# Moving a column minimum and the 1/l and h of two batches from VectorE to GpSimd in a fused attention and gated feed-forward kernel

## The chip, the cores and the metric

The kernel runs on one core of a Trainium2 chip. The metric is the device time of one execution in microseconds (us). A core has five engines that work side by side and wait for each other through semaphores: TensorE (PE in the profile, with its weight loads as PEld), VectorE (DVE), ScalarE (ACT), GpSimd (POOL) and SyncE (SP, which here only issues transfers). Each engine works through its own queue in the order in which the program wrote it.

## The reference

Two functions follow each other. The first is an attention through 32 inducing points, over 4 batches of 12416 tokens with 128 channels:

```python
def mab(q, kv):
    s = scale * (q @ kv.transpose(0, 2, 1))
    s = s - s.max(-1, keepdims=True)
    a = np.exp(s)
    a /= a.sum(-1, keepdims=True) + 1e-09
    return a @ kv
h = mab(I, x)          # stage 1: 32 points look at all tokens of a batch
return mab(x, h)       # stage 2: every token looks at the 32 points
```

The second is a gated feed-forward layer over all 49664 tokens, with 1536 hidden columns:

```python
gate = 1.0 / (1.0 + np.exp(-(x @ w_gate)))
val = x @ w_val
return (gate * val @ w_out).astype(np.float32)
```

## The kernel before, in words

Three things are interleaved. **The feed-forward steps** carry the program. The tokens go through in blocks of 512 (four chunks of 128). For each block 12 column groups of hidden values are made, in 8 steps that hold two groups (128x1024) and one group (128x512) in turn. For a step TensorE fills a gate tile and a value tile in PSUM (`hidden_mm`, L955), ScalarE takes the tanh of the gate tile (`gate`, L974), VectorE forms (t + 1) times the value tile (`product`, L987, written as `u`), and TensorE projects `u` with the output weights (`project`, L1018). The value and gate tiles have one PSUM buffer for the wide step and one for the narrow step. The weights of the gate and the values are folded with h beforehand: `hw_fill` (L426) multiplies h of a batch into both weight matrices, so that a block needs only the stage-2 probabilities of its tokens as the other operand.

**Stage 1 and stage 2 of later batches** run beside these steps, by a plan written out by hand. Two steps make a slot. `at(slot, f)` puts a piece of work behind the first step of a slot, and `at(slot, f, late=True)` behind the second. `beside` writes out what a slot has. A batch has 96 slots; in the code `b` counts from 0, and `o` is the first slot of the period in which the blocks of batch `b` go through. In that period the h of batch `b + 1` is made. The text calls the periods by their batches, 1 to 4.

- `plan_stage2` handles a group of 16 chunks: score by TensorE (`s2_score`, L533, which reads h as its moving operand), copy to SBUF by ScalarE (`s2_take`, L567), maximum and subtraction by a tree on GpSimd (`s2_lower_pool`, L577 to L584), exponential by ScalarE (`s2_exp_low`, L593), sum, inverse and product on GpSimd (`s2_sum_pool` L601, `s2_inverse_pool` L625 to L640, `s2_spread` L647), and a transposing transfer issued by SyncE (`s2_turn_dma`, L658). The inverse on GpSimd is a power with exponent -1 and one Newton step.
- `plan_combine` makes h of the next batch. Stage 1 leaves, for each row of 128, several columns of negated maxima (7 for batch 2, 5 for batches 3 and 4) and as many partial sums. `least` takes the minimum over the columns on VectorE (L469), and `join_min` joins the four row groups on GpSimd (L443 to L458). `weigh` makes the weights on ScalarE (L474), `join` adds the weighted sums on GpSimd (L485 to L493), `total` lets TensorE sum over the row groups into a PSUM tile `lh` (L505, L506) and takes the reciprocal of its l half on VectorE (L415), and the next slot multiplies the h half with it on VectorE (L420, `h_take`). The fills of `hw` follow 18 slots behind `join`.
- For batches 3 and 4 `least` stands at o + 44, `weigh` at o + 49, `join` at o + 54, `total` at o + 61, `h_take` at o + 62; for batch 2 at o + 52, 55, 56, 63 and 64.
- The first group of batch `b + 1` is scored in slots o + 67 and o + 68 (its `s2_score` is the first reader of the new h), copied at o + 70 and exponentiated at o + 78; the last group of batch `b` is copied at o + 58 and exponentiated at o + 66.
- `x_load` (L82) issues the input loads of batch `b + 2` from GpSimd's queue, in slots given at the end of the plan.

[...]

Of the kernel before, what the change touches and what calls it, by code (L numbers as in the profile page):

```python
# [9 lines left out]
F32 = mybir.dt.float32  # L10
# [3 lines left out]
ALU = mybir.AluOpType  # L14
AX = mybir.AxisListType

AFTER = mybir.DependencyInfo(mybir.DependencyClass.Sync, mybir.DependencyReason.DATA)
P = 128
GC = 16
# [7 lines left out]
def kernel(  # L27
# [9 lines left out]
    nc = tc.nc  # L37
    B, N, C = x.shape
    m = inducing.shape[0]
# [5 lines left out]
    NLO = NCH - NG * GC  # L45
# [10 lines left out]
    bp = ctx.enter_context(tc.tile_pool(name="bp", bufs=2))  # L56
    s1p = ctx.enter_context(tc.tile_pool(name="s1p", bufs=4))
    s2p = ctx.enter_context(tc.tile_pool(name="s2p", bufs=2))
    up = ctx.enter_context(tc.tile_pool(name="up", bufs=6))
    tp = ctx.enter_context(tc.tile_pool(name="tp", bufs=4))  # L60
    op = ctx.enter_context(tc.tile_pool(name="op", bufs=4))
# [12 lines left out]
    def x_load(b, s, first=0):  # L74
        c0, n = groups[s]
        if s == 0:
            c0, n = 0, n + NLO
        if b not in xn:
            xn[b] = xnp.tile([P, NCH, C], F16, tag="xn", name=f"xn_{b}")
        cuts = [c0, c0 + first, c0 + n] if first else [c0, c0 + n]  # L80
        for c, e in zip(cuts, cuts[1:]):
            nc.gpsimd.dma_start(xn[b][:, c:e, :], xv[b, :, c:e, :])  # L82
# [18 lines left out]
    def keep_on(n, tag):  # L101
# [14 lines left out]
        out=identf[:],  # L116
        in_=identf[:],
# [39 lines left out]
    minus1 = const.tile([P, GC + NLO], F32, tag="minus1")  # L157
# [36 lines left out]
    def at(slot, make, late=False):  # L194
        plan.setdefault((slot, late), []).append(make)
# [207 lines left out]
    hT16 = {}  # L403
# [9 lines left out]
    def l_inverse(l_ps):  # L413
        li = bp.tile([P, m], F32, tag="li")
        nc.vector.reciprocal(out=li[:], in_=l_ps)  # L415
        return li

    def h_take(b, h_ps, li):
        hT16[b] = bp.tile([P, m], F16, tag="hT", name="hT")
        nc.vector.tensor_tensor(out=hT16[b][:], in0=h_ps, in1=li[:], op=ALU.mult)  # L420

    def hw_fill(b, hf, tag):
        hw_ps = ps.tile([P, F // 4], F32, tag=tag, name="hw_ps")
# [37 lines left out]
    def plan_combine(b, lead, weights, joined, fill):  # L461
        q = b % 2
        nm1, hst = nm1s[q], hsts[q]
        st = {}
        ns = NS if b < 2 else NSH

        def least():
            ml = bp.tile([P, 1], F32, tag="ml")
            nc.vector.tensor_reduce(out=ml[:], in_=nm1[:, 0:ns], axis=AX.X, op=ALU.min)  # L469
            st["col"] = join_min(bp, ml)  # L470

        def weigh():
            st["w"] = bp.tile([P, NS], F32, tag="w1", name="w1")
            nc.scalar.activation(  # L474
                out=st["w"][:, 0:ns],
                in_=nm1[:, 0:ns],
                func=AF.Exp,
                bias=st["col"][:],
                scale=-1.0,
            )  # L480

        def join():
            assert summed[b] == ns
            hx = bp.tile([P, NS, C + 1], F32, tag="hx", bufs=1)
            nc.gpsimd.tensor_tensor(  # L485
                out=hx[:, 0:ns, :],
                in0=hst[:, 0:ns, :],
                in1=st["w"][:, 0:ns].unsqueeze(2).to_broadcast((P, ns, C + 1)),
                op=ALU.mult,
            )  # L490
            add_tree(hx, ns)
            e32l = bp.tile([P, m], F32, tag="e32l")
            nc.gpsimd.tensor_scalar(  # L493
                out=e32l[:],
                in0=e32[:],
                scalar1=hx[:, 0, C : C + 1],
                scalar2=TINY,
                op0=ALU.mult,
                op1=ALU.add,
            )  # L500
            st["hx"], st["e32l"] = hx, e32l

        def total():
            lh = ps.tile([P, 2, m], F32, tag="m", name="lh_ps")
            nc.tensor.matmul(lh[:, 0, :], ones[:], st["e32l"][:], start=True, stop=True)  # L505
            nc.tensor.matmul(lh[:, 1, :], st["hx"][:, 0, 0:C], e32[:], start=True, stop=True)  # L506
            st["lh"], st["li"] = lh, l_inverse(lh[:, 0, :])

        def part(hf):
            st["hw_ps"] = hw_fill(b, hf, "m")  # L510

        def keep(hf):
            if hf == 0:
                st["hwt"] = bp.tile([P, NI, P], F16, tag="hw", bufs=B, name="hwt")
            hw_take(st["hwt"], hf, st["hw_ps"])
            if hf == 1:
                hw[b] = st["hwt"]

        at(lead, least)
        at(weights, weigh)  # L520
        at(joined, join)
        at(joined + 7, total)
        at(joined + 8, lambda: h_take(b, st["lh"][:, 1, :], st["li"]))
        for hf, (first, second) in enumerate(fill):
            at(first, lambda hf=hf: part(hf))
            at(second, lambda hf=hf: keep(hf), late=True)
# [95 lines left out]
    def s2_inverse_pool(n, sme):  # L622
        rs = s2p.tile([P, GC + NLO], F32, tag="rs")
        near = s2p.tile([P, GC + NLO], F32, tag="near")
        nc.gpsimd.tensor_tensor(  # L625
            out=near[:, 0:n], in0=sme[:, 0:n], in1=minus1[:, 0:n], op=ALU.pow
        )
        off = s2p.tile([P, GC + NLO], F32, tag="off")
        nc.gpsimd.tensor_tensor(
            out=off[:, 0:n], in0=sme[:, 0:n], in1=near[:, 0:n], op=ALU.mult  # L630
        )
        nc.gpsimd.tensor_scalar(
            out=off[:, 0:n],
            in0=off[:, 0:n],
            scalar1=-1.0,
            scalar2=2.0,
            op0=ALU.mult,
            op1=ALU.add,
        )
        nc.gpsimd.tensor_tensor(  # L640
            out=rs[:, 0:n], in0=near[:, 0:n], in1=off[:, 0:n], op=ALU.mult
        )
        return rs[:, 0:n]

    def s2_spread(n, e, rs, eng):
# [94 lines left out]
    nm1, l1, hst = nm1s[0], l1s, hsts[0]  # L740
    for p in range(-2, NS - 3):
# [13 lines left out]
        if p == EARLY - 2:  # L755
            we = const.tile([P, EARLY], F32, tag="we")
            nc.vector.tensor_reduce(
                out=nml[:, 0:1], in_=nm1[:, 0:EARLY], axis=AX.X, op=ALU.min
            )
            nc.scalar.activation(  # L760
                out=we[:], in_=nm1[:, 0:EARLY], func=AF.Exp, bias=nml[:, 0:1], scale=-1.0
# [20 lines left out]
    c0, n = groups[sc]  # L782
# [3 lines left out]
    for j0, tag, copy in ((GC // 2, "v2", nc.scalar.copy), (GC - BC, "g1", nc.vector.tensor_copy)):  # L786
# [15 lines left out]
    ml = const.tile([P, 1], F32, tag="ml")  # L802
# [10 lines left out]
        out=top[:],  # L813
        in_=mlT_ps.rearrange("o (g r) -> o r g", g=4),
        axis=AX.X,
        op=ALU.min,
# [5 lines left out]
    for g in range(4):  # L822
# [19 lines left out]
        out=e32l[:], in0=e32[:], scalar1=lsum[:], scalar2=TINY, op0=ALU.mult, op1=ALU.add  # L842
# [5 lines left out]
        out=hw_parts[3],  # L848
# [195 lines left out]
    for b in range(B):  # L1044
        o = base[b]
        more = b + 1 < B

        if b == 0:
            plan_stage2(0, groups[1][0], o, None, o + 3, soon=True)
            plan_stage2(0, groups[2][0], o + 5, o + 7, o + 18)  # L1050
        for s in range(3 if b == 0 else 2, NG - 1):
            k = o + 16 * s - 28
            lag = k + 4 if b and more and s == 3 else None
            plan_stage2(b, groups[s][0], k, k + 2, k + (14 if more else 10), lag=lag)
        late = 2 if more and b else 0
        plan_stage2(b, groups[NG - 1][0], o + 56, o + 58, o + 66, far=o + 52 + late)
        if not more:
            continue
        single = (32, (47, 47, 47) if b else (43, 43, 43))
        if b == 0:  # L1060
            early = [(9, (16, 17, 17)), (13, (24, 24, 24))]
            later = [(25, (31, 31, 31)), (28, (35, 35, 35)), (40, (47, 48, 49)), (44, (50, 51, 51))]
            parts = dict(enumerate(early + later + [single]))
            turns = (5, 7, 17, 19, 22, 25, 20)
        else:
            parts = {2: (7, (16, 17, 17)), 3: (11, (18, 19, 19)), NG: single}
            turns = (-14, -5, -3, 2, 0, 8, 20)
            plan_shared(
                b + 1,
                o,  # L1070
                (-6, 2, 10, 14),
                (7, 11, 15),
                23,
                (26, 30, 42, 46),
                (40, 42, 49, 51),
                (45, 53),
            )
        for s, (score, total) in parts.items():
            plan_stage1(b + 1, s, o + score, [o + e for e in total])
        plan_combine(  # L1080
            b + 1,
            *((o + 44, o + 49, o + 54) if b else (o + 52, o + 55, o + 56)),
            [(o + 72, o + 74), (o + 80, o + 82)],
        )
        plan_stage2(b + 1, groups[0][0], o + 67, o + 70, o + 78)
        plan_stage2(b + 1, groups[1][0], o + 84, o + 86, o + 94)
        for g in range(NS):
            at(o + turns[g], lambda b=b, g=g: x_transpose_dma(b + 1, g))
            if b == 0 and 3 <= g < NG:
                at(o + 12, lambda g=g: x_load(1, g))  # L1090
        if b + 2 < B:
            for g in range(NG):
                at(o + (24 if b else 28, 33, 42, 60, 61, 68)[g], lambda b=b, g=g: x_load(b + 2, g))

    def beside(slot, late):
        for make in plan.pop((slot, late), ()):
# [53 lines left out]
```

## Time and profile before

| | |
|---|---|
| median of 3 runs | 720.13 us (718.76 to 720.21) |
| the profiled execution | 718.91 us |
| its span | 717.1 us, so 1.8 us lie around it |
| granted TensorE clock | 0.999 |
| VectorE busy | 699.7 us, 98% |
| ScalarE busy | 674.7 us, 94% |
| TensorE busy | 646.7 us, 90% |
| GpSimd busy | 438.8 us, 61% |

A row of a group gives: line, engine, operation, output<-inputs, shapes, count, then busy us and mean ns of one, then the engine's idle us just before them and what ended most of it. A row of the timeline gives start (us from the span's start), us, engine, line, operation, and in brackets idle time before it; it may hold several instructions in a row (xN), and what lies between two starts is what an instruction costs its engine, since an instruction can begin while the one before it is still writing.

### The profile page before, as it was taken

The page shows a single profiled execution, that of the slowest core. Times are in us where ns is not written, and L with a number is a line of the kernel's source. Part 1 is how long each engine was busy: PE and PEld are TensorE (multiplying, and loading weights), DVE is VectorE, ACT ScalarE, POOL GpSimd, SP SyncE. Part 2 cuts the span into 40 slices and gives each one's busy share as a digit, 9 for nine tenths or more (in the row PEclk, how much of TensorE's full clock was granted, in tenths as well). Part 3 has the DMA queues.
Part 4 walks back from the last instruction along what each step waited for, and adds up shares of the span by engine and source line. Part 5 has one row for each costly group of instructions (what it writes and reads, how often), then busy time and mean ns, then how long its engine had stood idle before and what let it go on. Part 6 is the DMA issues. An engine that isn't in the chain of part 4 may idle for free.

```text
span 717.1 us, 21610 instructions
## 1 busy us (share of the span) xinstructions
PE 646.7 (90%) x8478; PEld 392.2 (55%) x8478; DVE 699.7 (98%) x865; ACT 674.7 (94%) x1012; POOL 438.8 (61%) x739
## 2 busy tenths in 40 slices
PE   7989889999999989999998989999989899898887
PEld 4555555555555555655555556555555555555555
DVE  4799999999999999999999999999999999999998
ACT  4699999999999999999999999999999999999996
POOL 4464653878558988568657897486746556535100
PEclk9999999999999999999999999999999999999999
DMA  8979935263583245265485132221232123121211
GB/s 172 172 141 177 174 85 110 70 123 78 119 154 85 64 101 118 57 123 110 90 141 119 55 75 72 54 72 45 62 75 60 46 72 63 45 61 45 66 42 46
DMA packets 116726, 65.21 MB, mean 91 GB/s; under 512 B 99824, under 2 KB 101008, under 8 KB 116624
## 3 DMA queue, kind: packets, MB, share of 16 engines
q1 hardware_dynamic: 111936, 49.81, 31.1%
q0 software_dynamic: 4416, 13.90, 10.8%
q8 instruction: 66, 1.08, 0.7%
q14 instruction: 36, 0.29, 0.1%
q10 hardware_dynamic: 272, 0.13, 0.1%
HBM read 27.80 MB, written 25.43 MB: 74 GB/s over the span
## 4 chain that ended last, share of the span: by engine, by line
DVE 48%; issue 20%; PE 14%; ACT 11%; POOL 4%; DMA 2%; DVEq 1%; ACTq 0%; POOLq 0%
DVE u L987 46%; ACT t L974 10%; PE acc_ps L1018 6%; PE v_ps L955 5%; DMA xn<-in_x_dram 2%; POOL a2n L647 1%; DVE nm L229 1%; PE hp_ps L277 1%; POOL near L625 1%; DVEq L987 1%; POOL rise L577 1%; POOL sum L601 1%; POOL top L581 1%; PE g_ps L955 0%; ACT a1T L242 0%
## 5 line engine op out<-in xcount | busy, mean ns | idle before, releaser
L987 DVE SCALAR_TENSOR_TENSOR u<-t,v_ps 128x512 f16<-128x512 f16 (+1 forms) x778 | 675.0, 942 | 0.8 <-ACT t L974 0.7
L974 ACT ACTIVATE t<-g_ps 128x512 f16<-128x512 f32 (+1 forms) x777 | 592.4, 819 | 22.2 <-ACT t L974 12.3
L955 PE MATMUL v_ps<-a2r,hwt 32*128 32x512 f16 (+1 forms) x1188 | 293.5, 371 | 58.8 <-DVE u L987 57.9
L1018 PE MATMUL acc_ps<-wo,u 128*128 128x128 f16 x4656 | 327.5, 220 | 0.0
L1018 PEld LDWEIGHTS <-u 128*128 128x128 f16 x4656 | 261.0, 98 | 88.0 <-issue 87.1
L955 PE MATMUL g_ps<-a2r,hwt 32*128 32x512 f16 (+1 forms) x1188 | 296.7, 377 | 0.0
L955 PEld LDWEIGHTS <-hwt 32*128 32x128 f16 x2424 | 92.2, 91 | 189.4 <-issue 144.3
L647 POOL TENSOR_TENSOR a2n<-e,rs 128x2048 f16<-128x2048 f16 (+3 forms) x25 | 86.8, 3475 | 5.1 <-DVE rs L619 3.4
L601 POOL TENSOR_TENSOR sum<-e 128x256 f32<-128x256 f16 (+1 forms) x23 | 15.5, 672 | 114.6 <-ACT e L593 114.6
L625 POOL TENSOR_TENSOR near<-sme,minus 128x16 f32<-128x16 f32 (+1 forms) x22 | 65.2, 2963 | 1.7
L1036 ACT ACTIVATE o<-acc_ps 128x512 f32<-128x512 f32 x96 | 58.1, 605 | 0.0
L577 POOL TENSOR_TENSOR rise<-sc 128x256 f32<-128x256 f32 (+1 forms) x22 | 16.2, 739 | 40.3 <-ACT sc L567 40.0
L578 POOL TENSOR_SCALAR rise<-rise 128x256 f32<-128x256 f32 (+6 forms) x110 | 30.3, 275 | 9.7
L581 POOL TENSOR_TENSOR top<-top,rise 128x128 f32<-128x128 f32 (+3 forms) x88 | 28.5, 323 | 7.3
L601 POOL TENSOR_TENSOR sum<-sum 128x128 f32<-128x128 f32 (+3 forms) x92 | 28.5, 309 | 7.2
L577 POOL TENSOR_TENSOR rise<-top 128x128 f32<-128x128 f32 (+3 forms) x88 | 27.3, 310 | 6.9
L584 POOL TENSOR_TENSOR sc<-sc,top 128x512 f32<-128x512 f32 (+1 forms) x22 | 23.9, 1086 | 1.7
L533 PEld LDWEIGHTS <-xT 128*128 128x128 f16 x388 | 13.0, 96 | 11.5 <-issue 11.1
L82 POOL DMA_DIRECT2D xn<-in_x_dram x25 | 14.7, 596 | 6.5 <-DMA xn<-in_x_dram 5.6
L533 PE MATMUL s_ps<-hT,xT 128*128 128x32 f16 x388 | 18.0, 178 | 0.1
L581 POOL TENSOR_TENSOR top<-sc,rise 128x256 f32<-128x256 f32 (+1 forms) x22 | 16.2, 738 | 1.8
L363 POOL TENSOR_SCALAR xT<-xT,nm 128x512 f32<-128x512 f32 x8 | 15.8, 1994 | 0.2
(141 smaller groups left out, 273.0 us busy)
## 6 DMA issues: line engine op xcount, KB each, us to landing
out_dram<-o SPq DMA_DIRECT2D x96, 256.0 KB, 2.3
xn<-in_x_dram POOLq DMA_DIRECT2D x19, 512.0 KB, 7.9
xn<-in_x_dram POOLq DMA_DIRECT2D x4, 544.0 KB, 6.5
a2r<-a2n SPq DMA_TRANSPOSE x29, 4.4
xn<-in_x_dram POOLq DMA_DIRECT2D x1, 384.0 KB, 14.9
wg<-in_moe_w_gate_dram POOLq DMA_DIRECT2D x1, 384.0 KB, 16.3
wv<-in_moe_w_val_dram POOLq DMA_DIRECT2D x1, 384.0 KB, 16.5
wo<-in_moe_w_out_dram POOLq DMA_DIRECT2D x1, 384.0 KB, 16.0
```

Source lines behind the costliest of these rows:

```text
L533: nc.tensor.matmul(s2[:, j, :], xT[b][:, c + j, :], hT16[b][:], start=(j == 0), stop=whole and j == j1 - 1, skip_group_check=True,)
L577: nc.gpsimd.tensor_tensor(out=r, in0=far, in1=near, op=ALU.subtract)
L578: nc.gpsimd.tensor_scalar(out=r, in0=r, scalar1=BIG, scalar2=0.0, op0=ALU.min, op1=ALU.max)
L581: nc.gpsimd.tensor_tensor(out=top[:, 0:n, 0:w], in0=near, in1=r, op=ALU.add)
L601: nc.gpsimd.tensor_tensor(out=d[:, 0:n, :], in0=src[:, :, 0:w], in1=src[:, :, w : 2 * w], op=ALU.add)
L625: nc.gpsimd.tensor_tensor(out=near[:, 0:n], in0=sme[:, 0:n], in1=minus1[:, 0:n], op=ALU.pow)
L647: eng.tensor_tensor(out=a2n[:, 0:n, :, :], in0=e.unsqueeze(2).to_broadcast((P, n, 4, m)), in1=rs.unsqueeze(2).unsqueeze(3).to_broadcast((P ...
L955: st[what + "end"] = nc.tensor.matmul(pt[:, k, col : col + nb * P], hw[b][r : r + 32, j // 2, :], a2r[r : r + 32, o : o + nb, :].rearrange ...
L974: st["tanh"] = nc.scalar.activation(out=st["t"][:, :, c:e], in_=st["g"][:, :, c:e], func=AF.Tanh, scale=0.5)
L987: u = nc.vector.scalar_tensor_tensor(out=st["u"][:, :, c:e], in0=st["t"][:, :, c:e], scalar=1.0, in1=st["v"][:, :, c:e], op0=ALU.add, op1= ...
L1018: nc.tensor.matmul(acc[0][(i // 2) % len(acc[0])][:, i, :], st["u"][:, k, ts(i, P)], wo16[:, NI * (j % 2) + j // 2, :], start=(j == 0 and ...
L1036: nc.scalar.mul(out=o32[:], in_=acc[0][0][:], mul=0.5)
```

## The change

`least` forms the minimum over the columns on GpSimd for batches 2, 3 and 4: one tensor_scalar with two minima for every two further columns (three for 7 columns, two for 5), each reading the one before it. For batches 3 and 4 ScalarE copies the whole `lh` tile (128x64) to SBUF, behind the second step of slot o + 61, and GpSimd forms 1/l in the same four operations as in stage 2 and then multiplies h, where VectorE took the reciprocal and multiplied. The two input loads of the period of batch 2 that stood at o + 60 and o + 61 stand at o + 64 and o + 65. In the stage-2 inverse the intermediate tile is gone and its result is formed in place.

```diff
-    def h_take(b, h_ps, li):
+    def h_take(b, h_ps, li, eng=nc.vector):
         hT16[b] = bp.tile([P, m], F16, tag="hT", name="hT")
-        nc.vector.tensor_tensor(out=hT16[b][:], in0=h_ps, in1=li[:], op=ALU.mult)
+        eng.tensor_tensor(out=hT16[b][:], in0=h_ps, in1=li[:], op=ALU.mult)
+
+    def inverse_pool(out, x, near, minus):
+        nc.gpsimd.tensor_tensor(out=near, in0=x, in1=minus, op=ALU.pow)
+        nc.gpsimd.tensor_tensor(out=out, in0=x, in1=near, op=ALU.mult)
+        nc.gpsimd.tensor_scalar(
+            out=out, in0=out, scalar1=-1.0, scalar2=2.0, op0=ALU.mult, op1=ALU.add
+        )
+        nc.gpsimd.tensor_tensor(out=out, in0=near, in1=out, op=ALU.mult)
...
         def least():
             ml = bp.tile([P, 1], F32, tag="ml")
-            nc.vector.tensor_reduce(out=ml[:], in_=nm1[:, 0:ns], axis=AX.X, op=ALU.min)
+            src = nm1[:, 0:1]
+            for k in range(1, ns, 2):
+                nc.gpsimd.tensor_scalar(
+                    out=ml[:],
+                    in0=src,
+                    scalar1=nm1[:, k : k + 1],
+                    scalar2=nm1[:, k + 1 : k + 2],
+                    op0=ALU.min,
+                    op1=ALU.min,
+                )
+                src = ml[:]
             st["col"] = join_min(bp, ml)
...
-            st["lh"], st["li"] = lh, l_inverse(lh[:, 0, :])
+            st["lh"] = lh
+            if b < 2:
+                st["li"] = l_inverse(lh[:, 0, :])
+
+        def take():
+            if b < 2:
+                return h_take(b, st["lh"][:, 1, :], st["li"])
+            lh = bp.tile([P, 2, m], F32, tag="lh", name="lh", bufs=1)
+            nc.scalar.copy(out=lh[:], in_=st["lh"][:])
+            li = bp.tile([P, m], F32, tag="li")
+            near = bp.tile([P, m], F32, tag="near", bufs=1)
+            inverse_pool(li[:], lh[:, 0, :], near[:], minus1[:, 0:1].to_broadcast((P, m)))
+            h_take(b, lh[:, 1, :], li, nc.gpsimd)
...
-        at(joined + 8, lambda: h_take(b, st["lh"][:, 1, :], st["li"]))
+        at(joined + (8 if b < 2 else 7), take, late=b > 1)
...
     def s2_inverse_pool(n, sme):
         rs = s2p.tile([P, GC + NLO], F32, tag="rs")
         near = s2p.tile([P, GC + NLO], F32, tag="near")
...
+        inverse_pool(rs[:, 0:n], sme[:, 0:n], near[:, 0:n], minus1[:, 0:n])
         return rs[:, 0:n]
...
-                at(o + (24 if b else 28, 33, 42, 60, 61, 68)[g], lambda b=b, g=g: x_load(b + 2, g))
+                at(o + (24 if b else 28, 33, 42, 64 if b else 60, 65 if b else 61, 68)[g], lambda b=b, g=g: x_load(b + 2, g))
```

Inside `plan_combine` b is the batch whose h is made, so `b < 2` there is batch 2 (the first batch is made before the steps begin and takes another path); in the loads at the end b is the period's batch.

More of the change, by code (lines that the diff above doesn't have):

```diff
@@ L624, in s2_inverse_pool @@
         near = s2p.tile([P, GC + NLO], F32, tag="near")
[L625 to L642, printed above, removed]
+        inverse_pool(rs[:, 0:n], sme[:, 0:n], near[:, 0:n], minus1[:, 0:n])
         return rs[:, 0:n]
```

## The prediction

> **What bounds the kernel now.** I read the page's busy times first, then the costliest groups, then the timeline of each engine around the places that the change touches.
>
> ```profile
> PE 646.7 (90%) x8478; PEld 392.2 (55%) x8478; DVE 699.7 (98%) x865; ACT 674.7 (94%) x1012; POOL 438.8 (61%) x739
> ...
> L987 DVE SCALAR_TENSOR_TENSOR u<-t,v_ps 128x512 f16<-128x512 f16 (+1 forms) x778 | 675.0, 942 | 0.8 <-ACT t L974 0.7
> ...
> L955 PE MATMUL v_ps<-a2r,hwt 32*128 32x512 f16 (+1 forms) x1188 | 293.5, 371 | 58.8 <-DVE u L987 57.9
> ```
>
> VectorE is the bound: its products take 675.0 us and it stood idle 0.8 us before them in the whole run. TensorE waits for VectorE (57.9 us before the value fills), not the other way round. So each tenth of a us taken from VectorE's queue is a tenth gained, and each tenth in which VectorE has no filled value tile is lost for good, as it has no slack to catch up with. GpSimd is busy 61% of the time; what matters there is whether something is late at one place.
>
> **VectorE: what goes.** The view by tile gives the durations, VectorE's timeline what they cost in its queue.
>
> ```profile
> L469 DVE TENSOR_REDUCE ml<-nm x3: 140/141/153, 127.3 to 450.2; 128x1 f32<-128x5 f32 x2, 128x1 f32<-128x7 f32 x1
> L415 DVE RECIPROCAL li<-lh_ps x3: 347/347/347, 146.4 to 479.8; 128x32 f32<-128x32 f32 x3
> L420 DVE TENSOR_TENSOR hT<-lh_ps,li x3: 182/183/183, 148.4 to 481.8; 128x32 f16<-128x32 f32 x3
> ```
>
> ```profile
> 281.83 0.14 DVE L469 TENSOR_REDUCE ml<-nm 128x1 f32<-128x5 f32 x1
> 281.90 1.79 DVE L987 SCALAR_TENSOR_TENSOR u<-t,v_ps 128x512 f16<-128x512 f16 x2
> ...
> 311.33 0.35 DVE L415 RECIPROCAL li<-lh_ps 128x32 f32<-128x32 f32 x1
> 311.60 1.79 DVE L987 SCALAR_TENSOR_TENSOR u<-t,v_ps 128x512 f16<-128x512 f16 x2
> 313.31 0.18 DVE L420 TENSOR_TENSOR hT<-lh_ps,li 128x32 f16<-128x32 f32 x1
> 313.41 2.40 DVE L987 SCALAR_TENSOR_TENSOR u<-t,v_ps 128x512 f16<-128x512 f16 x3
> ```
>
> From start to next start a minimum costs 0.07 us, a reciprocal 0.27, a product h 0.10: the product behind starts while the small one still writes. Three minima, two reciprocals and two products make 3 x 0.07 + 2 x 0.37 = 0.95 us. By the full durations it would be 3 x 0.14 + 2 x (0.347 + 0.183) = 1.48; that is the upper end. I take 0.95, as the next start is what the queue feels.
>
> **GpSimd: what comes.** The groups by shape price the new operations.
>
> ```profile
> L625 POOL TENSOR_TENSOR near<-sme,minus 128x16 f32<-128x16 f32 x18 | 52.8, 2933 | 1.5
> L625 POOL TENSOR_TENSOR near<-sme,minus 128x17 f32<-128x17 f32 x4 | 12.4, 3101 | 0.2
> L577 POOL TENSOR_TENSOR rise<-top 128x32 f32<-128x32 f32 x18 | 4.3, 240 | 1.4
> L578 POOL TENSOR_SCALAR rise<-rise 128x32 f32<-128x32 f32 x18 | 3.9, 216 | 1.6
> L493 POOL TENSOR_SCALAR e32l<-e,hx 128x32 f32<-128x32 f32 x3 | 0.9, 297 | 0.3
> L444 POOL TENSOR_SCALAR quad<-quad 32x1 f32<-32x1 f32 x3 | 1.1, 375 | 0.3
> L567 ACT COPY sc<-s_ps 128x32 f32<-128x32 f32 x4 | 0.8, 206 | 0.0
> L292 ACT COPY hst<-hp_ps 128x129 f32<-128x129 f32 x10 | 2.9, 288 | 0.0
> ```
>
> The power is the dear one. One column more (16 to 17) adds 168 ns, so 2933 = 245 + 16 x 168, and for 32 columns I estimate 245 + 32 x 168 = 5.62 us. Bounds: 2.93 below (if more columns cost nothing, which the row of 17 speaks against) and 5.87 above (twice the 16). Then three products of 128x32 at 0.24, one tensor_scalar at 0.22 (0.30 by the dearer row), and four gaps of 0.08 (in the timeline below a tree step of 0.77 begins at 307.12 and the next at 307.97): 5.62 + 0.72 + 0.22 + 0.32 = 6.88 us from the start of the power to h.
>
> [...]
>
> Where does the chain stand in the queues? GpSimd's timeline for batch 3 and, behind the dots, batch 4:
>
> ```profile
> 307.12 0.77 POOL L577 TENSOR_TENSOR rise<-sc 128x272 f32<-128x272 f32 x1
> 307.97 0.41 POOL L578 TENSOR_SCALAR rise<-rise 128x272 f32<-128x272 f32 x1
> ...
> 313.88 1.13 POOL L584 TENSOR_TENSOR sc<-sc,top 128x544 f32<-128x544 f32 x1
> 314.95 1.20 POOL L82 DMA_DIRECT2D xn<-in_x_dram  x2
> 321.36 0.69 POOL L601 TENSOR_TENSOR sum<-e 128x272 f32<-128x272 f16 x1 [5.21 <-ACT e L593]
> ...
> 482.37 1.13 POOL L584 TENSOR_TENSOR sc<-sc,top 128x544 f32<-128x544 f32 x1
> 489.84 0.70 POOL L601 TENSOR_TENSOR sum<-e 128x272 f32<-128x272 f16 x1 [6.34 <-ACT e L593]
> ```
>
> And the first reader of h, on TensorE's timeline (slot o + 67), with ScalarE's copy that releases the tree:
>
> ```profile
> 306.44 0.59 ACT L567 COPY sc<-s_ps 128x512 f32<-128x512 f32 x1
> ...
> 320.45 0.39 PE L955 MATMUL v_ps<-a2r,hwt 32*128 32x512 f16 x2
> ...
> 320.78 0.36 PE L533 MATMUL s_ps<-hT,xT 128*128 128x32 f16 x8
> 321.08 0.39 PE L955 MATMUL v_ps<-a2r,hwt 32*128 32x512 f16 x1
> ...
> 321.40 0.84 PE L1018 MATMUL acc_ps<-wo,u 128*128 128x128 f16 x12
> 322.18 0.39 PE L955 MATMUL v_ps<-a2r,hwt 32*128 32x512 f16 x2
> ...
> 489.27 0.36 PE L533 MATMUL s_ps<-hT,xT 128*128 128x32 f16 x8
> ```
>
> The new chain is written at o + 61, behind the tree that ends at 315.01, and this tree begins at 307.12 because ScalarE's copy ends at 307.03: the change moves none of that. The loads are out of the way, so the power starts where they did, at 314.95. h is there at 314.95 + 6.88 = 321.83, and with some 0.1 for the semaphore TensorE can score at 321.93. It scored at 320.78, so it is 1.15 us late. For batch 4 the tree ends at 483.50: 483.45 + 6.88 + 0.1 = 490.43 against 489.27, 1.16 late. (TensorE would come there 0.37 earlier than before, by what VectorE saved; it stands some 1.5 us. The 0.37 is spent in that wait and may not be counted again.)
>
> **Does the wait reach VectorE?** Behind the scores in TensorE's queue stand the narrow value fill (321.08), twelve projections of 0.84 us and the next wide fill (322.18), back to back. VectorE has one wide product in hand when TensorE stops; then it needs the narrow fill, and 0.6 us later the wide one, which comes only after the projections. TensorE has at most about 0.05 us to spare in that stretch, so nearly all arrives: 2 x about 1.1 = 2.2 us.
>
> **The other parts.** ScalarE's copy of 128x64 lies between 0.21 and 0.29 us. It falls where ScalarE idled:
>
> ```profile
> 312.22 1.51 ACT L974 ACTIVATE t<-g_ps 128x1024 f16<-128x1024 f32 x2 [0.31 <-ACT t L974]
> ...
> 132.37 0.29 ACT L474 ACTIVATE w<-nm,top 128x7 f32<-128x7 f32 x1
> ...
> 341.40 0.63 ACT L593 ACTIVATE e<-sc 128x512 f16<-128x512 f32 x1
> ```
>
> It costs nothing while that cover of 0.31 stands, and at most 0.29 x 2 without. The minima on GpSimd take two or three tensor_scalars of about 0.375 + 0.1 (the row of L444 has the same two pointer operands). Where the margin is smallest, for batch 2, that is 1.4 us:
>
> ```profile
> 129.29 0.83 POOL L458 COPY top<-quad 32x1 f32<-32x1 f32 x4
> ...
> 339.22 1.07 POOL L584 TENSOR_TENSOR sc<-sc,top 128x512 f32<-128x512 f32 x1
> ...
> 332.67 4.24 SPq L658 DMA_TRANSPOSE a2r<-a2n  x2
> DMA to landing us min/median/max: 2.4/4.4/6.9
> ```
>
> `top` is done at 130.12 and would be at 131.5; ScalarE asks for it at 132.37. Hidden by 0.85 us. Without that cover ScalarE, with the tanh behind it, would wait for what is over.
>
> Behind the h chain in period 2 GpSimd also issues the two moved loads (1.20), so the sum that began at 321.36 begins at 321.83 + 1.2 = 323.1, 1.7 us later. The tree of the next group then ends at 342.0 instead of 340.29, and ScalarE's exponential, in its queue before tanh, wanted it at 341.40. But by then all queues run 1.1 later (342.5), so it is just covered. The transposes of the last group (issued at 332.67) move by 1.7 too: 334.4 + 4.4 to land is 338.8, and the first gate fill that needs them comes 12 slots of 1.755 us ((479.8 - 146.4) / 190 slots) behind 320.45, at 341.5. The moved loads bring batch 4's tokens, which the transposing transfers read first some 30 slots later. The in-place inverse has the same four operations: nothing.
>
> **Sum.** 2.2 for the two late h, less 3 x 0.07 for the minima (the other 0.74 is inside the 2.2): +2.0 us. The profiled execution of 718.91 (span 717.1 and 1.8 around it) becomes 720.9. It lies 1.2 below the median, so on the median I predict 720.13 + 2.0 = 722.1.
>
> **The rivals.**
> 1. *h comes in time.* The power would have to take 4.1 us or less (5.62 less the 1.5 that TensorE would stand); at about 4.6 gain and loss are even. The bound of 2.93 allows it, the row of 17 columns speaks against it. Then VectorE's 0.95 is the result: 719.2, or 718.65 if the full durations count. [...]
> 2. *The wait is partly absorbed.* A pair of products takes 1.71 us (311.60 to 313.31), about 1.1 of it the wide one. That one could begin when its fill of 320.45 was done, at 320.84; so the narrow fill, done at 321.47, was wanted at about 322.0, half a us later. If the projections didn't stand between the fills, 0.5 of each 1.15 would be hidden: 2 x 0.65 - 0.21 = +1.1, 721.2. Against it stands the back-to-back row of twelve. Chance 0.15.
> 3. *GpSimd's lateness spreads.* The dearer row for the tensor_scalar and the upper bound of the power add 0.33 to each batch, and if ScalarE's exponential at 341.40, the copy without its cover or the transposes with their 6.9 us landing bite too, 0.3 to 0.7 more: +3 to +3.9, some 723.5. Chance 0.15.
>
> **How the numbers follow.** The forecast holds 0.55, with 721.3 to 722.9 as its own range. A change within 0.2% (1.44 us) can hardly be told from none. Slower by more: nine tenths of the forecast and all of rival 3, 0.65. Within: the rest of the forecast, rival 2 and half of rival 1, 0.27. Faster by more: the other half, 0.08. The range runs from rival 1 to the end of rival 3: 719.1 to 724.0.
>
> **What would show it.** Right: a power of 128x32 near 5.6 us starting at the end of the 128x544 tree; TensorE idle some 1.5 us before the score in slot o + 67, twice, ended by GpSimd's h; VectorE's idle before the products up from 0.8 to about 4 us (the two waits of 1.5 plus what there was), while its busy time falls by one to one and a half us; no idle time of ScalarE before L474. Wrong: a power much below 5 us, or a wait on TensorE without one on VectorE.

## The result, and the profile after

The changed kernel takes 720.21 us (median of 22 runs, 720.02 to 721.66). The kernel before took 718.93 us beside it (22 runs). The ratio is 1.0014 with a 95% interval of 1.0008 to 1.0021: it is slower, by 1.0 us by the ratio and 1.3 by the medians, half to two thirds of the 2.0 us that were forecast, and less than the 0.2% that was set as the bound. The forecast of 722.1 was built on a median of 3 runs, 720.13, that was itself 1.2 us too high: the runs of the kernel before lie in two groups some 1.4 us apart (718.8 to 719.1 and 720.1 to 720.6, with one at 722.84), and two of those 3 were of the upper one. The profiled executions (718.91 and 720.26, spans 717.1 and 718.5) differ by 1.4 us.

The page of the kernel after, busy times and the costliest group:

```profile
PE 646.0 (90%) x8478; PEld 391.8 (55%) x8478; DVE 699.2 (97%) x858; ACT 674.9 (94%) x1014; POOL 453.0 (63%) x756
...
L1000 DVE SCALAR_TENSOR_TENSOR u<-t,v_ps 128x512 f16<-128x512 f16 (+1 forms) x778 | 674.9, 945 | 2.7 <-PE g_ps L968 2.0
```

VectorE's busy time fell by 0.5 us (699.7 to 699.2), and yet its idle time before the products went from 0.8 to 2.7 us, now ended by TensorE. GpSimd's timeline in the period of batch 2, where h of batch 3 is made:

```profile
313.81 1.13 POOL L614 TENSOR_TENSOR sc<-sc,top 128x544 f32<-128x544 f32 x1
314.89 5.43 POOL L423 TENSOR_TENSOR near<-lh,minus 128x32 f32<-128x32 f32 x1
320.40 0.25 POOL L424 TENSOR_TENSOR li<-lh,near 128x32 f32<-128x32 f32 x1
320.75 0.22 POOL L425 TENSOR_SCALAR li<-li 128x32 f32<-128x32 f32 x1
321.05 0.25 POOL L428 TENSOR_TENSOR li<-near,li 128x32 f32<-128x32 f32 x1
321.38 0.25 POOL L420 TENSOR_TENSOR hT<-lh,li 128x32 f16<-128x32 f32 x1
321.60 1.21 POOL L82 DMA_DIRECT2D xn<-in_x_dram  x2
322.82 0.71 POOL L631 TENSOR_TENSOR sum<-e 128x272 f32<-128x272 f16 x1
```

TensorE's timeline there, and (last row) in the period of batch 3:

```profile
320.31 0.39 PE L968 MATMUL v_ps<-a2r,hwt 32*128 32x512 f16 x2
...
321.68 0.35 PE L563 MATMUL s_ps<-hT,xT 128*128 128x32 f16 x8 [0.97 <-POOL hT L420]
321.96 0.39 PE L968 MATMUL v_ps<-a2r,hwt 32*128 32x512 f16 x1
...
322.29 0.84 PE L1031 MATMUL acc_ps<-wo,u 128*128 128x128 f16 x12
323.06 0.39 PE L968 MATMUL v_ps<-a2r,hwt 32*128 32x512 f16 x2
...
490.90 0.35 PE L563 MATMUL s_ps<-hT,xT 128*128 128x32 f16 x8 [0.97 <-POOL hT L420]
```

And VectorE's:

```profile
322.46 0.69 DVE L1000 SCALAR_TENSOR_TENSOR u<-t,v_ps 128x512 f16<-128x512 f16 x1 [0.47 <-PE g_ps L968]
323.51 1.22 DVE L1000 SCALAR_TENSOR_TENSOR u<-t,v_ps 128x1024 f16<-128x1024 f16 x1 [0.36 <-PE g_ps L968]
```

The mechanism is the one forecast. The power (GpSimd's row of 5.43 us) starts where the tree ends, h is there at 321.63, and TensorE stands for 0.97 us in front of the score, in both periods. VectorE waits twice: 0.47 for the narrow fill that stood behind the scores, 0.36 for the wide fill that stood behind the twelve projections.

Since the 778 products of VectorE are the same in all these kernels, their starts can be compared one by one. The table gives the steps of the difference to the kernel before (start of a product less the start of the same product before, us), worked out from the traces; `o` is here the first slot of the period in which the h of the batch is made:

| where | after |
|---|---|
| minimum, batches 2, 3, 4 | -0.07, -0.07, -0.07 |
| o + 61, where the reciprocal was: narrow product, then the wide one behind it (batch 3; 4) | -0.27, +0.27; -0.27, +0.27 |
| o + 62, where the product h was (batch 3; 4) | -0.10; -0.10 |
| o + 67, behind the late score: narrow, then wide product (batch 3; 4) | +0.56, +0.44; +0.55, +0.44 |
| o + 56, wide product (batch 4 alone) | -0.09 |
| five steps of 0.05 to 0.08, one of them upward, from slot 275 on, together | -0.19 |
| all steps under 0.035, together | +0.09 |
| end | +1.38 |

Each late h costs 1.0 us in waits; from ahead of o + 61 to behind the late wide product it is 0.89 (starts from -0.05 to +0.84 in batch 3, from +0.68 to +1.57 in batch 4), since the product h that left VectorE gives 0.10 back. The removed reciprocals gain nothing: what the narrow product gains, the next wide product loses.

### The profile page after: what moved, and what is told of

Read it like the earlier page. It is cut to its first block, busy times and chain, and to the rows that moved or that the text cites. A ratio compares the mean times of both kernels' runs of the same rounds, so it can differ in the third digit from the quotient of the medians.

```text
span 718.5 us, 21633 instructions
## 1 busy us (share of the span) xinstructions
PE 646.0 (90%) x8478; PEld 391.8 (55%) x8478; DVE 699.2 (97%) x858; ACT 674.9 (94%) x1014; POOL 453.0 (63%) x756
## 4 chain that ended last, share of the span: by engine, by line
DVE 47%; issue 20%; PE 15%; ACT 10%; POOL 4%; DMA 2%; DVEq 1%; ACTq 0%; POOLq 0%
DVE u L1000 46%; ACT t L987 9%; PE acc_ps L1031 7%; PE v_ps L968 6%; DMA xn<-in_x_dram 2%; POOL near L423 2%; DVE nm L229 1%; PE hp_ps L277 1%; DVEq L1000 1%; POOL top L611 1%; POOL rise L607 1%; PE g_ps L968 1%; POOL xn L82 0%; POOL rise L608 0%; POOL sc L614 0%
```

## The experiments

**The score one slot later and one slot earlier.** `score_68` and `score_66` move one number of the plan in the changed kernel, for batches 3 and 4:

```diff
-        plan_stage2(b + 1, groups[0][0], o + 67, o + 70, o + 78)
+        plan_stage2(b + 1, groups[0][0], o + (68 if b else 67), o + 70, o + 78)
```

(66 in place of 68 for the other); `before_score_68` makes the same move in the kernel before.

> The changed kernel, with the first group of batches 3 and 4 scored one slot later (o + 68 and o + 69). Theory L (the late h is the whole loss): h is there at 321.63, the score then stands at about 322.4, so TensorE's two waits of about 1 us go; what stays is VectorE's saving. Theory L with the reciprocal's place counted as a gap that TensorE's four sums leave anyway: 3 x 0.07 + 2 x 0.10 = 0.4 us below the kernel before. By the prediction's account (0.37 for each batch): 0.95 below. Rival (GpSimd's longer queue makes something else late): the time stays at that of the changed kernel, about 1.3 above before, with a new wait in place of the old one.

> The changed kernel, with that score one slot earlier (o + 66 and o + 67). Theory L: TensorE waits a whole slot longer, 1.0 + 1.73 us in each of the two periods, and all of it reaches VectorE: about 2 x 1.7 = 3.4 us above the changed kernel, 4.7 above before (ratio 1.0065). If TensorE's wait is partly absorbed by filled tiles (rival 2 of the prediction), at most 2 x 1.2 above the changed kernel.

> The kernel before, with the same score one slot later. Both theories: no change (within 0.2 us in the profile), since h was 7 us early there. If the later slot itself costs or saves something, this run shows it, and the comparison with the run of the changed kernel at o + 68 has to be corrected by it.

`score_68`: 718.85 against 718.96 us, ratio 1.0004 (0.9993 to 1.0015). Both waits in front of the score are gone (TensorE's timeline, batch 3; h is there 0.8 us ahead):

```profile
322.28 0.36 PE L563 MATMUL s_ps<-hT,xT 128*128 128x32 f16 x8
```

The steps at o + 61 (-0.27, +0.27) and o + 62 (-0.10) are as in the changed kernel, so the account of the reciprocal as a gain falls. A new step of +0.57 has come near 343 us, in the period of batch 2 alone, and the end is at -0.17. So the second rival of the expectation holds in part: GpSimd's longer queue does make something else late. ScalarE's and GpSimd's timelines show what it is:

```profile
341.69 0.63 ACT L623 ACTIVATE e<-sc 128x512 f16<-128x512 f32 x1 [0.47 <-POOL sc L614]
```

```profile
340.59 1.07 POOL L614 TENSOR_TENSOR sc<-sc,top 128x512 f32<-128x512 f32 x1
```

GpSimd's tree ends at 341.66, and the exponential, in ScalarE's queue ahead of the tanh, waits for it. In the changed kernel this wait was hidden: the tree ends there at 341.75, nearly at the same time, but ScalarE asks for it at 342.23 only, since VectorE's products run 0.84 us late by then.

`before_score_68`: 718.81 us, ratio 0.9996 (0.9982 to 1.0011); no step larger than 0.035 at any product, except 1.56 before the first one. That one was there at 18.5 us, long before the score that was moved: TensorE waited 2.30 us for an input load, 0.63 in the kernel before. The later slot costs nothing.

`score_66`: 727.98 us, ratio 1.0122 (1.0106 to 1.0137), 9 us above before, where 4.7 were expected. (Its profiled execution, 728.68 us, also came 1.4 us late out of its start, as that of `min_only` did; the last section shows it.) TensorE's wait grew as expected, by one slot, but what followed it cost more:

```profile
323.06 0.35 PE L563 MATMUL s_ps<-hT,xT 128*128 128x32 f16 x8 [2.73 <-POOL hT L420]
```

The view by stages (stage, its length, busy times of PE, PEld, DVE, ACT and POOL with their instructions, then the granted TensorE clock, DMA share and GB/s):

```profile
320.00:324.50 4.50, 1.77 (x30) 1.21 (x29) 2.28 (x3) 2.11 (x4) 3.85 (x7) 1.00 0.27 56
324.50:328.00 3.50, 3.50 (x33) 1.75 (x32) 1.98 (x4) 2.04 (x4) 2.51 (x7) 0.51 0.92 170
490.00:495.20 5.20, 2.35 (x31) 1.42 (x29) 3.83 (x5) 3.63 (x6) 4.87 (x5) 1.00 0.13 50
495.20:502.00 6.80, 6.71 (x61) 4.10 (x61) 3.51 (x4) 3.61 (x6) 4.07 (x8) 0.50 0.01 2
502.00:506.00 4.00, 3.64 (x48) 2.26 (x46) 3.96 (x6) 3.89 (x7) 3.67 (x5) 1.00 0.17 66
```

Behind each pause of 2.73 us the granted clock is 0.5, for 3.4 us in batch 3's case and 6.8 us in batch 4's. In these stages TensorE is busy nearly throughout (3.50 of 3.50 us and 6.71 of 6.80), VectorE 1.98 of 3.50 and 3.51 of 6.80. The whole loss at these two places, from the table of starts, is 4.0 and 5.0 us, against 1.0 each in the changed kernel.

**The minimum alone.** `min_only` is the kernel before with the new `least` and nothing else.

> The kernel before, with only the minimum over the columns on GpSimd (batches 2, 3 and 4). The prediction and theory L: 3 x 0.07 = 0.2 us less in the profile, steps of 0.07 at the three places; too little for the timed ratio (0.9997). Rival (the reductions stood in gaps like the reciprocal): no step at all. Rival (the weights are late): ScalarE idle before L474 and about 0.5 us more.

718.90 us, ratio 0.9997 (0.9989 to 1.0006). Steps of -0.08, -0.07 and -0.07 at the three places: the reductions were no gap filler, and the gain is there, though only the trace can show it. On GpSimd the first operation of a minimum took 0.38 us and the others 0.36, near the 0.375 of the forecast. ScalarE had no idle time before the weights, in this kernel and in the changed one (row of ScalarE's timeline of the kernel after, batch 2; `top` was done at 131.46):

```profile
132.37 0.29 ACT L492 ACTIVATE w<-nm,top 128x7 f32<-128x7 f32 x1
```

**The loads behind the tree.** `score_68_loads_80` is `score_68` with `80 if b else 60, 81 if b else 61` in place of `64 if b else 60, 65 if b else 61`.

> The changed kernel with the score at o + 68 and the two loads of period 2 moved further, to o + 80 and o + 81. With the score at o + 68 alone one new wait had come, of 0.57 us in VectorE's queue near 343 us, where ScalarE's exponential waited for GpSimd's tree. If the 1.2 us of the two loads ahead of that tree are its cause, the wait is gone and the profile's span is 0.57 shorter: about 0.75 us below the kernel before, ratio 0.9990. If the lateness comes from the h chain alone, at least half of the wait stays.

718.29 us against 718.94, ratio 0.9991 (0.9978 to 1.0005). The profile's span is 716.4 us, 0.7 below the kernel before, and the steps add up to -0.68. The exponential comes without a wait, and the page has VectorE's idle time back near its old value:

```profile
341.16 0.63 ACT L623 ACTIVATE e<-sc 128x512 f16<-128x512 f32 x1
```

```profile
L1000 DVE SCALAR_TENSOR_TENSOR u<-t,v_ps 128x512 f16<-128x512 f16 (+1 forms) x778 | 674.5, 942 | 1.1 <-ACT t L987 0.7
```

So without the loads, 1.21 us of GpSimd's queue, the tree is in time, even behind the long power. This kernel beats both the kernel before and the changed one by its median and its trace; the interval of its ratio to the kernel before still holds 1.

**The loads ahead of the power.** `loads_60` is the changed kernel with the loads at `60, 61` as before.

> The changed kernel with the two loads of period 2 back at o + 60 and o + 61, ahead of the power in GpSimd's queue. Theory L: in batch 3 alone TensorE waits 1.2 us longer (2.2 instead of 1.0), and 1.2 us more reach VectorE: 1.2 above the changed kernel. In the run with the score at o + 66 a pause of 2.7 us was followed by 3.4 us at half the clock, which cost 1.2 more; if 2.2 us are enough for that, it is 2.4 above. Rival: the loads are hidden anyway, no change.

725.13 us, ratio 1.0072 (1.0052 to 1.0092): 5 us above the changed kernel, not 1.2 or 2.4. The pause in front of batch 3's score is 2.24 us, 1.27 longer than in the changed kernel, as forecast. Then (TensorE's timeline, and the view by stages with the clock behind the busy times):

```profile
322.92 0.37 PE L563 MATMUL s_ps<-hT,xT 128*128 128x32 f16 x8 [2.24 <-POOL hT L420]
323.22 0.60 PE L968 MATMUL v_ps<-a2r,hwt 32*128 32x512 f16 x1
```

```profile
320.00:322.50 2.50, 0.68 (x10) 0.37 (x8) 1.96 (x3) 2.02 (x4) 2.25 (x4) 1.00 1.01 220
322.50:332.80 10.30, 9.88 (x88) 6.13 (x88) 6.14 (x7) 5.99 (x9) 9.40 (x14) 0.50 0.42 90
332.80:337.00 4.20, 3.66 (x46) 2.04 (x42) 3.84 (x6) 3.81 (x7) 3.86 (x6) 1.00 0.00 0
```

The clock is halved for 10.3 us, and VectorE is busy 6.14 of them. The steps at this place add up to 5.5 us, 4.5 more than in the changed kernel: 1.3 by the longer pause, and the 3.2 that remain fall in these 10.3 us, in which TensorE is busy 9.88 and VectorE waits for it. The expectation had allowed 1.2 for the clock. That the loads were moved in the change is thus worth 4 to 5 us.

**Half the power.** `half_power` leaves half of the power out: it runs over 16 of the 32 columns, and the other 16 start from a constant.

```diff
+    near_all = const.tile([P, m], F32, tag="near_all")
+    nc.vector.memset(near_all[:], 1.0e-4)
...
+            nc.gpsimd.tensor_tensor(
+                out=near[:, 0:part], in0=x[:, 0:part], in1=minus, op=ALU.pow
+            )
```

> The changed kernel with the power of batches 3 and 4 over 16 of the 32 columns (the other half of 1/l starts from a constant; that part of the computation is left out), score and loads as in the change. Theory L: the power takes 2.94 instead of 5.43 us, h is there at about 319.1, 1.5 us ahead of the score at o + 67, and both waits go, as does the lateness behind them: about 0.4 us below before in the profile. If something else than the length of the power made h late, the waits stay.

718.25 us, ratio 0.9985 (0.9972 to 0.9998). GpSimd's timeline:

```profile
314.77 2.91 POOL L429 TENSOR_TENSOR near_all<-lh,minus 128x16 f32<-128x16 f32 x1
...
318.73 0.25 POOL L420 TENSOR_TENSOR hT<-lh,li 128x32 f16<-128x32 f32 x1
318.95 1.21 POOL L82 DMA_DIRECT2D xn<-in_x_dram  x2
321.06 0.69 POOL L641 TENSOR_TENSOR sum<-e 128x272 f32<-128x272 f16 x1 [0.89 <-ACT e L633]
```

h is there at 318.98, GpSimd waits for ScalarE again before the sum, and the steps of the waits are gone: of those in the table above, the ones behind the late score are missing in both periods, the others remain, and the end is at -0.75 (0.10 of it from the start of the run). The length of the power is the cause of both late h. The late tree of `score_68` needed both, the long power and the loads behind it: it is in time here, with the loads where the change puts them.

**Without the reciprocals.** `no_recip` is the kernel before with a constant in place of 1/l for batches 3 and 4, so the division by l is left out there.

> The kernel before, with the two reciprocals of batches 3 and 4 on VectorE left out (a constant stands for 1/l; the division by l is left out there). The prediction's account: 2 x 0.27 = 0.54 us less. Theory G (the reciprocal fills a gap that TensorE's four sums for l and h leave, since the next wide value fill comes late): a step of -0.27 at the narrow product and +0.27 at the wide one behind it, nothing in the end.

718.90 us, ratio 0.9998 (0.9985 to 1.0011). The steps are -0.27 at the narrow product and +0.27 at the wide one behind it, in both batches, and nothing else changes after the start. VectorE's timeline:

```profile
313.56 1.22 DVE L990 SCALAR_TENSOR_TENSOR u<-t,v_ps 128x1024 f16<-128x1024 f16 x1 [0.16 <-PE g_ps L958]
```

In place of the reciprocal stands a wait for TensorE's wide fill. In slot o + 61 TensorE has the four fp32 sums for l and h between its fills. Its timeline in the kernel before, and below it the same wide fill in `no_recip`, whose run came 1.40 us late out of its start:

```profile
310.06 0.41 PE L505 MATMUL lh_ps<-e32l,ones 128*128 128x32 f32 x2
310.31 0.39 PE L506 MATMUL lh_ps<-e,hx 128*128 128x32 f32 x2
...
310.94 0.84 PE L1018 MATMUL acc_ps<-wo,u 128*128 128x128 f16 x12
311.72 0.39 PE L955 MATMUL v_ps<-a2r,hwt 32*128 32x512 f16 x2
```

```profile
313.12 0.39 PE L958 MATMUL v_ps<-a2r,hwt 32*128 32x512 f16 x2
```

Less the 1.40 us the fill starts at 311.72 in both: it does not move when the reciprocal goes. The reciprocal was free.

## Why the prediction was right and wrong

- *VectorE is the bound, and what it waits is lost.* Right: the waits of 0.47 and 0.36 stay to the end in the table of starts.
- *The chain is 6.88 us and starts at 314.95.* It started at 314.89 and h was there at 321.63, 6.74 us later. The estimate for the power (5.62) was 0.19 too high (the small operations and gaps took 0.05 more than forecast): the measured cost from 16 to 32 columns is (5.43 - 2.93) / 16 = 156 ns a column, not the 168 that the step from 16 to 17 gave. The row of 17 was a difference of two means over one column and was stretched sixteen times.
- *0.1 us for the semaphore.* It was the author's estimate; measured it was 0.05 (321.63 to 321.68).
- *h is 1.15 us late, 1.1 of it reaches VectorE, in each batch: 2.2 us.* This is the step that failed: the term of the two late h was too large. Against the score of the kernel before, the score was 0.90 late (321.68 against 320.78), and the wide product behind it 0.84 late (323.51 against 322.67 in the two traces). The 0.25 us between 1.15 and 0.90 are 0.06 of the start of the chain, 0.14 of its length and 0.05 of the semaphore. By the table of starts the term is 2 x 0.89 = 1.78 us, so that it explains 0.4 of the 0.6 us between the forecast of +2.0 and the +1.38 of the traces; the small steps named under "The rest" are the other 0.2.
- *Nearly all of the wait arrives.* Right, and rival 2 fell: TensorE stood 0.97 us, and VectorE lost 0.56 + 0.44. VectorE's idle time rose to 2.7 us and not to about 4, as that was counted from two waits of 1.5.
- *A reciprocal costs VectorE's queue 0.27 us.* Wrong as a gain: the start-to-start time of 0.27 is right, but the queue behind it would have waited as long for TensorE. In the sum this did no harm, because the prediction had spent the 0.37 of a reciprocal and a product h inside TensorE's wait. It shows in the length of that wait: TensorE came to the score 0.07 us earlier than before and not 0.37, and stood 0.97 instead of 1.5. It also shows in rival 1, which counted on 0.95 us once h is in time: the steps at the minima and the products h give 3 x 0.07 + 2 x 0.10 = 0.41, and the ends of `score_68_loads_80` and `half_power`, -0.68 and -0.75, hold small steps that were not counted on.
- *The tree of the next group is just covered, because all queues run late by then.* Right: with the cover gone and the loads still ahead of it, in `score_68`, it cost 0.57 us.
- *ScalarE's copy is hidden, the minima are hidden, the transposes and the in-place inverse cost nothing.* The copy took 0.26 us, within the bounds, and no step is found at it. No step is found at the others either.
- *The rest.* The -0.09 at o + 56 of batch 4 and the -0.19 from slot 275 on were not foreseen. They are there in all kernels with the whole change and in neither `min_only` nor `no_recip`. VectorE's timeline names no wait at these places, before or after; which part of the change brings them was not tried, and their cause stays open.
- *Rival 1, h in time by a power of 4.1 us or less (its chance was 0.15).* It fell: the power took 5.43 us, in both periods.
- *What the chances said.* Slower by more than 0.2% had 0.65; the measured 0.14% lies in the case that had 0.27. The sum by rows gave +2.0; the steps of the starts give 2 x 0.99 - 3 x 0.07 - 2 x 0.10 - 0.09 - 0.19 = +1.29 and, with the steps too small to list, +1.38, and the runs +1.0 (0.0014 x 718.9) to +1.28 (between the medians). The upper end of rival 3 does not come out of its terms, which add up to 2.0 + 2 x 0.33 + 0.7 = +3.4 and not +3.9; the measured time lies far below either.

## What to carry to other kernels

When work moves to an engine that takes longer for it (here 6.74 us on GpSimd against 0.35 and 0.18 for the reciprocal and the product h on VectorE), find its first reader and count back: here the reader stood 6 slots behind the start of the chain, one slot too near, and one number in the plan was worth more than all the operations that were moved off the busy engine. An operation on the bound engine is worth its time only if the next operation was ready (without the reciprocal, `no_recip`, one product gained 0.27 us and the next lost them); look at what feeds the one behind it. And a delay may cover another one, so that mending the first shows the second.

## What the runs showed of the hardware

In these runs a pause of TensorE was not always paid by its length alone. After 0.97 us (the changed kernel, twice) the granted clock stayed at 1.00; after 2.24 us (`loads_60`) and 2.73 us (`score_66`, twice) it was 0.5 for 10.3, 3.4 and 6.8 us, about three, one and two times the same length.

Nor did the length of the pause alone decide. The 2.30 us that TensorE stood at the start of `before_score_68` are longer than the 2.24 of `loads_60`, and its clock stayed at 1.00 (0.999 over the whole span). What makes the clock fall, and what decides between 3.4 and 10.3 us, was not shown: no run set the pause or the busy time ahead of it on purpose.

In three profiled executions (`min_only`, `no_recip` and `score_66`) the clock also falls for 3.4 us just after the feed-forward steps begin. In `min_only` no such pause stands in the 4.40 us ahead of it: TensorE was busy 3.81 of them. The view by stages of `min_only`, and below it that of the kernel before:

```profile
30.00:34.40 4.40, 3.81 (x52) 1.87 (x53) 3.73 (x8) 3.93 (x6) 2.46 (x3) 1.00 0.46 91
34.40:37.90 3.50, 3.50 (x33) 2.05 (x32) 2.86 (x4) 2.28 (x4) 1.06 (x3) 0.51 0.59 112
```

```profile
34.40:37.90 3.50, 3.50 (x50) 1.98 (x48) 3.50 (x5) 2.81 (x5) 0.93 (x3) 1.00 0.59 112
```

There the products fall 1.5 us behind, before any changed instruction runs. It is not the only way to lose as much at the start: the execution of `before_score_68` came 1.56 us late by the wait for an input load, at full clock. With differences of this size, starts compared product by product told more than the timed ratios.
